# A gated FFT convolution followed by an MLP: two subtractions of its first part moved from GpSimd to VectorE

## The chip, the cores and the metric

The kernel runs on one core of one Trainium2 chip. The metric is the device time of one execution in microseconds. Each core has engines with a queue of their own, which take their instructions in the order of the program: TensorE (PE, with weight loads shown as PEld), VectorE (DVE), ScalarE (ACT), GpSimd (POOL), and SyncE (SP), which here issues nearly all DMAs. Data lie in SBUF; matrix products come out in PSUM, from where VectorE and ScalarE read them.

## The reference

Two stages. The first is a long convolution along the sequence with a filter that a small network makes from position embeddings; the second an MLP with ELU.

```python
def _attn_ref(x, v, pos_emb, w1, w2):            # x, v: 4 x 12480 x 128
    h_filt = (np.maximum(pos_emb @ w1, 0.0) @ w2) * np.exp(-0.01 * pos)[:, None]
    u = x * v
    Uf = np.fft.rfft(u, n=2 * S, axis=1)
    Hf = np.fft.rfft(h_filt, n=2 * S, axis=0)
    y = np.fft.irfft(Uf * Hf[None], n=2 * S, axis=1)[:, :S]
    return x * y

def _moe_ref(x, w_in, w_out):                    # 49920 x 128, 128 x 2048, 2048 x 128
    h = x @ w_in
    return np.where(h > 0, h, np.exp(np.minimum(h, 0)) - 1) @ w_out
```

## The kernel before

**Split numbers.** Products that need float32 accuracy are made from operands in a shorter format, `F32R`. An operand is split in two: the high part is a copy into `F32R`, the low part what the copy lost (`low = full - high`). `mm3` (L52 to L55) then does three matmuls: high by high (L53), low by high (L54) and high by low (L55). `copy` (L57) is always a ScalarE activation, so all high parts are shown at L58.

**The order of the work.** The schedule is written out by hand: each engine's queue holds its instructions in the order in which the Python code makes them. The transform over 12480 positions is done in two steps over 104 x 60. The kernel has three parts: `stage1` for batch 0 with `first=True`, in which the filter and the MLP's weights are prepared as well; `stage2` for batch 0 with `first=True`; and then the MLP over all batches, with `stage1` and `stage2` of batches 1 to 3 (with `first=False`) interleaved.

**The first part.** `stage1(..., first=True)` is a loop over 15 groups g, each with four steps i (r = i // 2, w = i % 2). What a group needs was prepared ahead:

- `load(g + 3)` at i = 0 (L182): two DMAs, `xt` and `vt`, of 416 KB each, in three buffers.
- `gate(g + 2)` at the group's start (L147): `vt = xt * vt`. It runs on VectorE for groups 0 and 1, on GpSimd afterwards (L101, L102).
- `split(g + 1)` at i = 1 (L184): `u_h` on ScalarE (L110), then `u_l = vt - u_h` (L112).

In each of its steps a group runs three matmuls `aps` from `u_h`, `u_l` (L158). Their result is copied out of PSUM by VectorE when w = 0 (L161) and by ScalarE when w = 1 (L163), and two steps together are stored by one DMA.

Between these lies the filter (class `Filter`), for q = 2g + r. `step(q + 3, 0)` transposes the embeddings (`pt`), `step(q + 2, 1)` multiplies by w1 (`rp`) and takes the Relu on ScalarE (`r_sb`, L236), `step(q + 1, 2)` multiplies by w2 (`hps`, L242), applies the window on VectorE (`h_sb`, L245), and splits: `h_h` on ScalarE (L252) and `h_l = h_sb - h_h` (L253). `transform(q)` runs twelve matmuls `Hps` on an earlier step's `h_h`, `h_l`, then combines on ScalarE (`hsb`, L266) and VectorE (L267).

At i = 1 `weights(c)` decodes 256 columns of the MLP's weights, which arrive as 64 bit numbers, with ten operations on VectorE (seven at L301, then L315, L317 and L318). `split_w(c - 1)` then splits the columns decoded one round earlier: the high part on ScalarE, the low part on GpSimd (L329). `split(g + 1)` follows.

So the queues hold, for one group:

| step | PE | VectorE | ScalarE | GpSimd |
| --- | --- | --- | --- | --- |
| start | | | | gate(g + 2) L102 |
| i = 0 | pt, aps, hps | L161, L245 | pt_sb, h_h | h_l L253 |
| i = 1 | rp, aps, Hps | L267, ten of weights | r_sb, a_sb, hsb, weights high, u_h | weights low L329, u_l L112 |
| i = 2 | pt, aps, hps | L161, L245 | pt_sb, h_h | h_l L253 |
| i = 3 | rp, aps, Hps | L267 | r_sb, a_sb, hsb | |

Before the loop, `gate(0)`, three rounds of `step`, `gate(1)` and `split(0)` come in this order. In `stage1` with `first=False` the choice at L111 is VectorE already.

Of the kernel before, what the change touches and what calls it, by code (L numbers as in the profile page):

```python
# [11 lines left out]
ALU = mybir.AluOpType  # L12
# [26 lines left out]
def fftconv_gate_elu_mlp_kernel(ctx: ExitStack, tc: tile.TileContext, x, v, pos_emb, w1, w2,  # L39
                                w_in, w_out, dft, ident, window, tab, out):  # L40
    nc = tc.nc
# [15 lines left out]
    def copy(out, in_):  # L57
        nc.scalar.activation(out=out, in_=in_, func=ACTF.Copy)  # L58
# [22 lines left out]
    def stage1(st, h, ps_pool, ps_tag, first):  # L81
# [22 lines left out]
        def split(g):  # L104
            if g >= NG:
                return
            vt = ld.pop(g)[1]
            u_h = up.tile([N1, 2, G, D], F32R, tag="u_h", name="u_h")
            u_l = up.tile([N1, 2, G, D], F32R, tag="u_l", name="u_l")
            copy(u_h, vt)  # L110
            e = nc.gpsimd if first and g else nc.vector  # L111
            e.tensor_tensor(out=u_l, in0=vt, in1=u_h, op=ALU.subtract)  # L112
            us[g] = (u_h, u_l)

# [18 lines left out]
        else:  # L133
# [6 lines left out]
            for _ in range(2 if h > 1 else 0):  # L140
                yield
        split(0)
        if not first:
            yield
        for g in range(NG):
# [3 lines left out]
            for i in range(4):  # L149
# [33 lines left out]
                if i == 1:  # L183
                    split(g + 1)  # L184
# [9 lines left out]
    class Filter:  # L194
# [25 lines left out]
        def step(self, g, q):  # L220
            if g >= NGF:
                return
            hp, psh = self.hp, self.psh
            if q == 0:
                p = self.pos.pop(g)
                pt = psh.tile([64, 2 * GF, N1], F32, tag="t", name="pt")
                for n in range(2 * GF):
                    nc.tensor.transpose(out=pt[:, n, :], in_=p[:, n // GF, n % GF, :], identity=id_sb[:N1, :N1])
                pt_sb = hp.tile([64, 2 * GF, N1], F32, tag="pt_sb", name="pt_sb", bufs=2)
                copy(pt_sb, pt)  # L230
                self.t[g] = pt_sb
            elif q == 1:
                rp = psh.tile([64, 2 * GF, N1], F32, tag="r", name="rp")
                nc.tensor.matmul(out=rp, lhsT=self.w1, rhs=self.t[g], start=True, stop=True)
                r_sb = hp.tile([64, 2 * GF, N1], F32, tag="r_sb", name="r_sb", bufs=2)
                nc.scalar.activation(out=r_sb, in_=rp, func=ACTF.Relu)  # L236
                self.t[g] = r_sb
            elif q == 2:
                r_sb = self.t.pop(g)
                hps = psh.tile([N1, 2, GF, D], F32, tag="h", name="hps")  # L240
                for n in range(2 * GF):
                    nc.tensor.matmul(out=hps[:, n // GF, n % GF, :], lhsT=r_sb[:, n, :], rhs=self.w2,  # L242
                                     start=True, stop=True)
                h_sb = hp.tile([N1, 2, GF, D], F32, tag="h_sb", name="h_sb", bufs=2)
                nc.vector.tensor_tensor(  # L245
                    out=h_sb, in0=hps,
                    in1=self.win[:, :, g * GF:(g + 1) * GF].rearrange("p w (n o) -> p w n o", o=1).to_broadcast([N1, 2, GF, D]),
                    op=ALU.mult)
                h_h = hp.tile([N1, 2, GF * D], F32R, tag="h_h", name="h_h", bufs=2)
                h_l = hp.tile([N1, 2, GF * D], F32R, tag="h_l", name="h_l", bufs=2)  # L250
                hv = h_sb.rearrange("p w n d -> p w (n d)")
                copy(h_h, hv)  # L252
                nc.gpsimd.tensor_tensor(out=h_l, in0=hv, in1=h_h, op=ALU.subtract)  # L253
                self.hs[g] = (h_h, h_l)

        def transform(self, g):
# [499 lines left out]
```

## Time and profile before

| | |
| --- | --- |
| median of 3 runs | 3546.19 us (3544.32 to 3550.76) |
| the profiled execution | 3553.1 us |
| its span, first to last instruction | 3551.3 us |
| mean granted TensorE clock | 0.981 |
| busy in the span: PE, DVE, ACT, POOL | 96%, 88%, 68%, 66% |
| DMA | 646.30 MB, mean 182 GB/s |

The span counts from the first instruction to the last; the execution's time has a little more around it. Busy shares are means over parts with different limits. The granted clock is the share of full speed at which TensorE was let run; it is 1.0 or 0.5 at any time, and means over a stretch lie between. In the rows below times are microseconds from the span's start, unless marked ns; a row of a timeline gives start, duration, engine, line, operation, output and inputs, and in brackets how long the engine sat idle before it and whose end released it.

### The profile page before, as it was taken

How to read it: one execution, taken by the hardware profiler on the slowest of the kernel's cores; microseconds unless marked ns; L12 is line 12 of the kernel's file. 1: busy time of each engine (PE TensorE's matmuls, PEld its weight loads, DVE VectorE, ACT ScalarE, POOL GpSimd, SP SyncE). 2: the span in 40 equal slices, each digit the busy share in tenths (PEclk: the TensorE clock that was granted, in tenths of full speed). 3: DMA queues.
4: the chain of work that ended last, by engine and by line, in shares of the span. 5: the costliest groups of instructions: out<-in, count | busy, mean ns of one | idle time of the engine just before them, and what ended most of it. 6: DMA issues, size and time to landing. Idle time of an engine off the chain costs nothing.

```text
span 3551.3 us, 53404 instructions
## 1 busy us (share of the span) xinstructions
PE 3394.7 (96%) x18444; PEld 3131.3 (88%) x18444; DVE 3114.3 (88%) x3897; ACT 2410.1 (68%) x3290; POOL 2355.2 (66%) x1622
## 2 busy tenths in 40 slices
PE   7978879999999999999999999999999999999999
PEld 5667758889989998889999998899999999999998
DVE  4549969999999989999999989999999988888887
ACT  3445548766666677876666677776666677777776
POOL 5758857667767766557677656666766656565565
PEclk9879979999999999999999999999999999999999
DMA  6758887667767616778888846778888832222221
GB/s 187 236 170 268 269 245 222 203 175 217 214 191 215 192 50 182 242 213 228 230 241 225 230 124 183 239 215 237 232 240 226 230 102 60 71 59 64 67 59 27
DMA packets 383995, 646.30 MB, mean 182 GB/s; under 512 B 24678, under 2 KB 170438, under 8 KB 374366
## 3 DMA queue, kind: packets, MB, share of 16 engines
q1 hardware_dynamic: 383305, 642.73, 63.8%
q8 instruction: 147, 2.41, 0.3%
q14 instruction: 122, 1.00, 0.1%
q10 hardware_dynamic: 421, 0.16, 0.0%
HBM read 412.76 MB, written 230.03 MB: 181 GB/s over the span
## 4 chain that ended last, share of the span: by engine, by line
PE 59%; DVE 10%; DMA 7%; issue 4%; ACT 1%; POOL 1%; SPq 1%; POOLq 0%; DVEq 0%; ACTq 0%
PE fps L53 8%; PE fps L55 8%; PE fps L54 8%; PE ops L53 7%; PE ops L54 7%; PE ops L55 7%; DMA al<-a_d 3%; DVE g_l L581 3%; PE bps L450 3%; DVE g L572 2%; DMA vt<-in_v_dram 2%; PE xps L53 2%; PE xps L55 2%; PE xps L54 2%; PE yps L53 1%
## 5 line engine op out<-in xcount | busy, mean ns | idle before, releaser
L575 POOL CAST g_h<-g 128x832 fp32r<-128x832 f32 x960 | 1228.3, 1283 | 961.0 <-DVE g L572 960.1
L565 ACT ACTIVATE n<-fps 128x832 f32<-128x832 f32 x960 | 831.9, 867 | 737.9 <-PE fps L55 725.1
L572 DVE SCALAR_TENSOR_TENSOR g<-n,fps 128x832 f32<-128x832 f32 x960 | 974.4, 1015 | 224.2 <-ACT n L566 218.2
L581 DVE TENSOR_TENSOR g_l<-g,g_h 128x832 fp32r<-128x832 f32 x960 | 1111.4, 1158 | 18.3 <-POOL g_h L575 18.3
L566 ACT ACTIVATE n<-n 128x832 f32<-128x832 f32 x960 | 864.6, 901 | 30.4
L53 PE MATMUL fps<-t_h,wi_h 128*128 128x416 f32 x1920 | 715.8, 373 | 22.1 <-DVE g L572 20.9
L53 PE MATMUL ops<-g_h,wo_h 128*128 128x416 f32 x1920 | 677.9, 353 | 0.8 <-ACT o_sb L58 0.3
L54 PE MATMUL ops<-g_l,wo_h 128*128 128x416 f32 x1920 | 675.2, 352 | 0.7 <-DVE g_l L581 0.7
L55 PE MATMUL fps<-t_h,wi_l 128*128 128x416 f32 x1920 | 675.8, 352 | 0.0
L55 PE MATMUL ops<-g_h,wo_l 128*128 128x416 f32 x1920 | 675.8, 352 | 0.0
L54 PE MATMUL fps<-t_l,wi_h 128*128 128x416 f32 x1920 | 675.0, 352 | 0.0
L431 POOL TENSOR_TENSOR p<-p 120x768 f32<-120x768 f32 x204 | 478.9, 2348 | 77.9 <-DVE p L425 58.4
L53 PEld LDWEIGHTS fps<-t_h,wi_h 128*128 128x128 f32 x1920 | 362.4, 189 | 55.9 <-DVE g L572 36.1
L54 PEld LDWEIGHTS fps<-t_l,wi_h 128*128 128x128 f32 x1920 | 364.4, 190 | 13.3 <-DVE t_l L554 0.3
L53 PEld LDWEIGHTS ops<-g_h,wo_h 128*128 128x128 f32 x1920 | 361.8, 188 | 7.1 <-POOL g_h L575 2.1
L54 PEld LDWEIGHTS ops<-g_l,wo_h 128*128 128x128 f32 x1920 | 362.5, 189 | 4.2 <-DVE g_l L581 1.4
L55 PEld LDWEIGHTS ops<-g_h,wo_l 128*128 128x128 f32 x1920 | 361.5, 188 | 4.1
L55 PEld LDWEIGHTS fps<-t_h,wi_l 128*128 128x128 f32 x1920 | 361.8, 188 | 3.2
L423 DVE TENSOR_TENSOR p<-xps,f 120x512 f32<-120x512 f32 x416 | 283.0, 680 | 14.1 <-DMA f<-f_d 5.1
L432 POOL TENSOR_TENSOR p<-p 120x256 f32<-120x256 f32 x204 | 249.5, 1223 | 16.0
L450 PE MATMUL bps<-p,t 120*120 120x256 f32 x832 | 220.4, 387 | 35.4 <-POOL p L432 26.6
L358 DVE TENSOR_TENSOR tl<-t,th 120x360 fp32r<-120x360 f32 x208 | 211.2, 1016 | 27.4 <-ACT th L58 27.3
(96 smaller groups left out, 4946.2 us busy)
## 6 DMA issues: line engine op xcount, KB each, us to landing
a_d<-a_sb SPq DMA_DIRECT2D x90, 832.0 KB
al<-a_d SPq DMA_DIRECT2D x156, 480.0 KB
f<-f_d SPq DMA_DIRECT2D x312, 240.0 KB
b_d<-b_sb SPq DMA_DIRECT2D x156, 480.0 KB
b<-b_d SPq DMA_DIRECT2D x90, 832.0 KB
t<-in_tab_dram SPq DMA_DIRECT2D x208, 281.2 KB
xt<-in_x_dram SPq DMA_DIRECT2D x60, 416.0 KB
vt<-in_v_dram SPq DMA_DIRECT2D x60, 416.0 KB
```

What stands on the lines that cost most here:

```text
L53: nc.tensor.matmul(out=ps, lhsT=hi, rhs=bh, start=start, stop=False)
L54: nc.tensor.matmul(out=ps, lhsT=hi, rhs=bl, start=False, stop=False)
L55: nc.tensor.matmul(out=ps, lhsT=lo, rhs=bh, start=False, stop=stop)
L423: nc.vector.tensor_tensor(out=p[:, :, :2], in0=ps[:, :, 0:1, :].to_broadcast([RI, TG, 2, D]), in1=f[:, :, r], op=ALU.mult)
L431: e.tensor_tensor(out=q, in0=q, in1=p, op=ALU.add)
L432: e.tensor_tensor(out=q[:, :, 1], in0=q[:, :, 1], in1=q[:, :, 2], op=ALU.add)
L450: nc.tensor.matmul(out=ps[:, o], lhsT=t[:, o, 3 * N2:], rhs=y[:, o, :2], start=True, stop=True)
L565: nc.scalar.activation(out=n, in_=ps[:, :, :NT], func=ACTF.Relu, scale=-1.0)
L566: nc.scalar.activation(out=n, in_=n, func=ACTF.Exp, scale=-1.0)
L572: nc.vector.scalar_tensor_tensor(out=g, in0=n, scalar=-1.0, in1=ps[:, :, :NT], op0=ALU.add, op1=ALU.max)
L575: nc.gpsimd.tensor_copy(out=g_h, in_=g)
L581: nc.vector.tensor_tensor(out=g_l, in0=g, in1=g_h, op=ALU.subtract)
```

## The change

The low part of `u` in the first part, groups 1 to 14, and the low part of the filter, 30 times, are computed by VectorE in place of GpSimd. Operands and results are the same, and each instruction keeps its place in the order of the program, now in VectorE's queue: `u_l` behind the ten operations of `weights`, `h_l` behind `h_sb` (L245). GpSimd keeps the gates (L102) and the weights' low parts (L329) in this part.

```diff
@@ split(g) in stage1
             copy(u_h, vt)
-            e = nc.gpsimd if first and g else nc.vector
+            e = nc.vector
             e.tensor_tensor(out=u_l, in0=vt, in1=u_h, op=ALU.subtract)
@@ step(g, 2) in Filter
                 copy(h_h, hv)
-                nc.gpsimd.tensor_tensor(out=h_l, in0=hv, in1=h_h, op=ALU.subtract)
+                nc.vector.tensor_tensor(out=h_l, in0=hv, in1=h_h, op=ALU.subtract)
```

## The prediction

> **What bounds the kernel now.** The profiled execution has a span of 3551.3 us and took 3553.1 us; the three timed runs have their median at 3546.19. The change touches only the first part, so I read stages by windows first, then who waits there, then one group as a timeline.
>
> ```profile
> 25.00:222.00 197.00, 182.63 (x908) 129.26 (x908) 105.15 (x238) 89.69 (x171) 147.24 (x71) 0.87 0.65 200
> ```
>
> The columns are stretch, length, busy time of PE, PEld, DVE, ACT and POOL, granted clock, DMA share and GB/s. The loop of 15 groups lasts from about 25 to 222 us. PE is busy 182.6 of 197 us, at a clock of 0.87; VectorE has 92 us free, GpSimd 50. DMA is no bound at 0.65. The next part starts with loads of what this one stores last, so a microsecond here is a microsecond of the whole.
>
> ```profile
> ACT h_h L58 <- DVE h_sb L245: 85.2, 30, 5.6
> PE aps L54 <- POOL u_l L112: 9.0, 10, 2.0
> ```
>
> Of the waits up to 240 us these two matter (sum in us, times, longest). PE waits 9.0 us for `u_l` from GpSimd: that is all the change can save directly. But ScalarE hangs on VectorE through `h_sb` 30 times, and VectorE is where the work goes.
>
> ```profile
> 81.40:92.90 11.50, 10.65 (x65) 7.58 (x64) 6.68 (x17) 6.12 (x14) 10.39 (x5) 1.00 0.85 268
> 92.90:106.35 13.45, 12.60 (x63) 9.38 (x63) 6.70 (x17) 6.26 (x13) 10.38 (x5) 0.80 0.81 259
> 106.35:121.05 14.70, 14.70 (x67) 10.23 (x65) 6.78 (x17) 6.38 (x13) 10.38 (x5) 0.72 0.71 226
> 132.60:148.20 15.60, 13.11 (x63) 9.39 (x63) 8.96 (x17) 6.25 (x13) 9.73 (x5) 0.80 0.72 225
> ```
>
> Each window is one group. At full clock it takes 11.5 us; a spell at half clock makes two neighbours 13.45 and 14.70, that is 28.15 - 2 x 11.52 = 5.1 us too long.
>
> ```profile
> 199.37 0.69 DVE L267 TENSOR_TENSOR hsb<-Hps,hsb 104x512 f32<-104x512 f32 x1 [3.02 <-ACT hsb L58]
> 199.72 3.02 POOL L329 TENSOR_TENSOR wo_l<-r,wo_h 128x256 fp32r<-128x256 f32 x1 [1.34 <-ACT wo_h L58]
> ...
> 202.18 0.85 DVE L318 TENSOR_TENSOR r<-r,k 128x256 f32<-128x256 f32 x1
> 202.70 2.56 POOL L112 TENSOR_TENSOR u_l<-vt,u_h 104x1024 fp32r<-104x1024 f32 x1
> 202.95 0.68 DVE L161 COPY a_sb<-aps 104x512 f32<-104x512 f32 x1
> 203.55 0.68 DVE L245 TENSOR_TENSOR h_sb<-hps,win_sb 104x512 f32<-104x512 f32 x1
> 204.26 0.63 ACT L58 ACTIVATE h_h<-h_sb 104x512 fp32r<-104x512 f32 x1 [3.28 <-DVE h_sb L245]
> 204.79 0.49 ACT L236 ACTIVATE r_sb<-rp 64x416 f32<-64x416 f32 x1
> 205.31 0.47 PE L54 MATMUL aps<-u_l,dft_h 104*104 104x512 f32 x1 [0.85 <-POOL u_l L112]
> 205.95 0.91 PEld L242 LDWEIGHTS hps<-w_sb,r_sb 64*104 64x104 f32 x8 [0.38 <-ACT a_sb L58]
> 206.28 0.69 DVE L267 TENSOR_TENSOR hsb<-Hps,hsb 104x512 f32<-104x512 f32 x1 [2.06 <-ACT hsb L58]
> ...
> 210.89 0.69 DVE L267 TENSOR_TENSOR hsb<-Hps,hsb 104x512 f32<-104x512 f32 x1 [2.72 <-ACT hsb L58]
> ```
>
> A clean group, L267 to L267, 11.52 us (start, length, engine, line). Two things meet at `hps` at 205.95. **One** is PE's own path, held 0.85 us at 205.31 by `u_l`, which left GpSimd at 205.26. **The other** is a chain through two queues: ten weight operations on VectorE up to L318, then L161, L245, then on ScalarE `h_h` and `r_sb`, which ends at 205.28 and feeds `hps`. It is only 0.7 us ahead of PE. Had PE not waited for `u_l`, `hps` would have started at 205.28 + 0.06, 5.97 after L267, and the rest, 210.89 - 205.95 = 4.94, would follow. So the group takes 10.9 + s, where s is whatever is put on VectorE ahead of L161.
>
> **The trace has tested this rule.**
>
> ```profile
> 132.44 0.69 DVE L267 TENSOR_TENSOR hsb<-Hps,hsb 104x512 f32<-104x512 f32 x1 [2.76 <-ACT hsb L58]
> 134.61 0.82 DVE L315 SCALAR_TENSOR_TENSOR r<-l,f 128x256 f32<-128x256 uint32 x1
> 135.11 2.57 POOL L112 TENSOR_TENSOR u_l<-vt,u_h 104x1024 fp32r<-104x1024 f32 x1
> 135.35 2.61 DVE L317 TENSOR_TENSOR k<-k,s 128x256 uint32<-128x256 uint32 x1
> 138.34 0.69 DVE L161 COPY a_sb<-aps 104x512 f32<-104x512 f32 x1
> ...
> 140.74 1.12 PE L242 MATMUL hps<-w_sb,r_sb 64*104 64x128 f32 x8 [2.29 <-ACT r_sb L236]
> ```
>
> Here L161 starts 5.90 after L267 instead of 3.58, so s = 2.32, and `hps` should start 5.97 + 2.32 = 8.29 after it; it starts at 8.30, PE now waiting for `r_sb`. What caused it: L317, two SBUF operands and 256 elements, took 2.61 us and ended when GpSimd's `u_l` did. The two engines don't run such operations side by side.
>
> **The change, part by part.** Durations:
>
> ```profile
> L112 DVE TENSOR_TENSOR u_l<-vt,u_h x46: 1208/1565/2457, 26.5 to 2334.8; 104x1024 fp32r<-104x1024 f32 x46
> L395 DVE TENSOR_TENSOR a_l<-al,a_h 120x512 fp32r<-120x512 f32 x1 | 0.7, 691 | 2.9 <-ACT a_h L58 2.9
> L253 POOL TENSOR_TENSOR h_l<-h_sb,h_h x30: 1264/1276/1514, 25.6 to 221.3; 104x512 fp32r<-104x512 f32 x30
> L102 POOL TENSOR_TENSOR vt<-xt,vt x12: 2346/2366/2559, 50.6 to 191.7; 104x1024 f32<-104x1024 f32 x12
> ```
>
> *`h_l`, 30 times, cost nothing.* It leaves GpSimd (1.28 us) and takes about 0.69 on VectorE, by the row of `a_l`, of equal width. In the queue it stands behind L245 and waits there for `h_h`, ready at 204.89; it would run to 205.6, while the next, L267, comes at 206.28 after 2.06 us of idling. Behind the waiting `h_l` are L267 and the next L161, both later anyway. If that cover were gone, 30 x 0.6 = 18 us. Before the loop the first `h_l` now precedes the second gate and the first `u_l`: between nothing and 0.63 + 0.69 = 1.3 us; I take 0.6.
>
> *`u_l`, 14 times, is on the chain.* It stands between L318 and L161. Alone it takes 1.21 us, less the 0.08 by which successive records overlap: s = 1.13 and a group of 12.03, **+0.5 us**. PE's 9.0 us of waiting for `u_l` are in this balance: `r_sb` is simply late instead.
>
> *The gate, moved without being edited.* On GpSimd the next operation behind L329 was `u_l`; now it is the gate L102 of a later group, and it reads SBUF too. It would ask for its operands in the same place, while L318 runs, and compete with VectorE's `u_l`. At 135.11 GpSimd's operation, recorded 0.32 before L315's end, went ahead of the following L317. At 202.70 it is 0.33 before L318's end. The opposite case exists:
>
> ```profile
> 598.44 1.54 DVE L112 TENSOR_TENSOR u_l<-vt,u_h 104x1024 fp32r<-104x1024 f32 x1
> 599.43 3.75 POOL L529 TENSOR_TENSOR b<-b,b 104x1024 fp32r<-104x1024 f32 x1 [0.53 <-ACT b L58]
> 599.90 1.01 DVE L581 TENSOR_TENSOR g_l<-g,g_h 128x832 fp32r<-128x832 f32 x1
> ```
>
> There VectorE's next operation ran at once and GpSimd waited. If the gate goes first, it ends where `u_l` did, at 205.26, and VectorE's `u_l` ends four times 0.28 later (L317, with a quarter of its elements, ended 0.28 after GpSimd at 137.68): 206.38. L161 starts 0.08 before that, at 206.30: s = 3.35, a group of 14.2, **+2.7 us**. [...]
>
> Is the gate ready by then?
>
> ```profile
> 99.99 1.62 SPq L94 DMA_DIRECT2D vt<-in_v_dram  x1
> 106.53 3.00 POOL L329 TENSOR_TENSOR wi_l<-r,wi_h 128x256 fp32r<-128x256 f32 x1 [2.99 <-ACT wi_h L58]
> 113.25 2.37 POOL L102 TENSOR_TENSOR vt<-xt,vt 104x1024 f32<-104x1024 f32 x1
> ```
>
> Its loads are issued at 99.99; with the store ahead of them they are 1.25 MB, about 5 us at 259 GB/s, so they land between 105 and 113.25, and L329 ends at 109.53. The trace leaves it open; I count half of the groups each way. The first and the last two have no such gate.
>
> *The clock.* PE's gap at `hps` grows from 0.85 to about 1.5 us, with the gate first to over 3.
>
> ```profile
> 213.70:217.10 3.40, 1.85 (x14) 1.49 (x13) 2.05 (x3) 1.32 (x3) 3.40 (x3) 1.00 0.31 91
> 217.10:222.00 4.90, 4.90 (x18) 3.60 (x17) 1.98 (x3) 1.90 (x4) 1.61 (x2) 0.50 0.58 162
> ```
>
> PE idled 1.55 of 3.4 us, and 0.50 was granted next; in the group from 81.40 it idled 0.85 and kept 1.00. Clock 0.87 over the loop is some 50 us at half, about five spells. I add two, at 2.4 (15.60 less 10.9 + 2.32) to 5.1 us: +7. At half clock PE is last (14.70 above 14.2), and the chain is hidden.
>
> **The sum.** Three uncontested groups 3 x 0.5 = 1.5; of eleven contested four late gates, 2.0, four early ones, 10.8, three hidden by half clock, 0; clock 7; head 0.6: **+22 us**. On the profiled execution that is 3575; on the median **3568 us**.
>
> **Rivals.** *The gate always goes first* (chance 0.2): 11 x 2.7 + 1.5 + six more spells at 3.5 = +52, 3598. For it speaks 135.11, against it 598.44. *The gate always comes too late, no more spells* (0.2): 11 x 0.5 = +6, 3552, no change. *Hidden altogether* (0.08): half clock or DMA sets the pace; 3546; the DMA share of 0.65 speaks against it. *Faster* (0.1): `u_l` is ready sooner, PE's gap closes and spells go. That decides where s is below 0.62 (11.52 - 10.9), or where spells fall away by luck of their timing: 9 us of waits and two or three spells, -19, 3527. Against it stand 1.13 for s and the 8.30 at 140.74. [...]
>
> **How the numbers follow.** The forecast has 0.42. About 0.2% (7 us) is what a measurement can tell from no change. Slower by more: forecast, first rival and a little of the second, 0.65; same 0.24; faster 0.11. The range takes in the late gate, less one spell, and most of the always early gate: 3547 to 3595.
>
> **What would show it.** Right: group windows of 12 to 14 us at full clock, PE waiting at `hps` for `r_sb` and no longer at L54; VectorE's `u_l` at 1.2 or 3.3 us, the long ones ending 1.1 after a gate; `h_l` followed by an idle VectorE; a clock below 0.87. Wrong: groups under 11.5 us, or L161 starting within 3.6 us of L267.

## The result and the profile after

| | us |
| --- | --- |
| before, median of 4 runs | 3548.48 (3544.32 to 3559.18) |
| after, median of 4 runs | 3592.74 (3589.06 to 3595.22) |
| ratio of after to before, 95% interval | 1.0119 (1.0094 to 1.0144) |
| forecast, range | 3568, 3547 to 3595 |

The kernel became 44 us slower. The direction was right and the time lies inside the range, but the forecast loss of 22 us was half of the real one; the time is near that of the first rival, in which the gate always goes first (3598).

The first fence is from the page of after, the second holds windows of after: the stretch behind the loop, the eleven contested groups together, one of them, and the two clock stretches within it (columns as in the prediction).

```profile
span 3590.2 us, 53421 instructions
```

```profile
262.00:3590.20 3328.20, 3202.34 (x17512) 2996.91 (x17510) 3008.75 (x3658) 2316.94 (x3114) 2211.36 (x1547) 0.99 0.64 181
53.70:240.10 186.40, 157.92 (x698) 111.06 (x697) 125.31 (x209) 68.89 (x133) 60.81 (x22) 0.75 0.56 176
121.35:138.30 16.95, 13.82 (x65) 9.64 (x65) 11.41 (x19) 6.26 (x13) 5.54 (x2) 0.80 0.56 164
...
124.90:131.60 6.70, 3.57 (x27) 2.79 (x25) 5.32 (x5) 1.98 (x5) 2.34 (x1) 1.00 0.17 54
131.70:138.40 6.70, 6.70 (x24) 4.78 (x23) 2.61 (x5) 2.66 (x6) 0.00 (x0) 0.50 0.80 205
```

The same two windows of before:

```profile
222.00:3551.30 3329.30, 3203.43 (x17511) 2997.66 (x17510) 3006.34 (x3656) 2315.93 (x3112) 2207.79 (x1548) 0.99 0.64 181
...
54.20:199.40 145.20, 136.15 (x698) 96.68 (x696) 76.32 (x177) 68.75 (x133) 113.83 (x56) 0.85 0.71 222
```

Behind the loop nothing changed: 3328 against 3329 us. The whole loss is in the first part, and nearly all of it in the eleven contested groups, 186.4 against 145.2 us: 16.95 a group instead of 13.2. GpSimd's busy time fell by half, VectorE's rose by 49 us (an operation that is held up counts as busy for all of its time, as the 3.40 us of `u_l` below), and PE did the same 698 matmuls in 41 us more.

The timeline of after shows one such group, the answer to the clean group of before:

```profile
121.35 0.69 DVE L267 TENSOR_TENSOR hsb<-Hps,hsb 104x512 f32<-104x512 f32 x1 [4.15 <-ACT hsb L58]
121.70 3.02 POOL L329 TENSOR_TENSOR wi_l<-r,wi_h 128x256 fp32r<-128x256 f32 x1 [12.23 <-ACT wi_h L58]
...
124.16 0.84 DVE L318 TENSOR_TENSOR r<-r,k 128x256 f32<-128x256 f32 x1
124.68 2.56 POOL L102 TENSOR_TENSOR vt<-xt,vt 104x1024 f32<-104x1024 f32 x1
124.92 3.40 DVE L112 TENSOR_TENSOR u_l<-vt,u_h 104x1024 fp32r<-104x1024 f32 x1
128.25 0.68 DVE L161 COPY a_sb<-aps 104x512 f32<-104x512 f32 x1
128.38 0.47 PE L54 MATMUL aps<-u_l,dft_h 104*104 104x512 f32 x1 [1.52 <-DVE u_l L112]
...
130.28 0.69 DVE L253 TENSOR_TENSOR h_l<-h_sb,h_h 104x512 fp32r<-104x512 f32 x1 [0.76 <-ACT h_h L58]
130.70 1.22 PE L242 MATMUL hps<-w_sb,r_sb 64*104 64x128 f32 x8 [1.61 <-ACT r_sb L236]
...
131.64 0.69 DVE L267 TENSOR_TENSOR hsb<-Hps,hsb 104x512 f32<-104x512 f32 x1 [0.67 <-ACT hsb L58]
...
138.30 0.69 DVE L267 TENSOR_TENSOR hsb<-Hps,hsb 104x512 f32<-104x512 f32 x1 [3.33 <-ACT hsb L58]
```

The gate is recorded at 124.68, right where GpSimd's `u_l` used to be, 0.32 before L318's end. VectorE's `u_l` takes 3.40 us and ends at 128.32, 1.08 after the gate's end at 127.24. That is what is called a collision below. L161 starts 6.90 after L267, s = 3.32. PE waits twice, 1.52 us for `u_l` and 1.61 for `r_sb`, and in the following 6.7 us its clock is 0.50, which stretches the other half of the group. All eleven contested `u_l` look like that; the three without a gate behind L329 take 1.21 to 1.22. The first and the last of the eleven in after's timeline:

```profile
57.23 3.39 DVE L112 TENSOR_TENSOR u_l<-vt,u_h 104x1024 fp32r<-104x1024 f32 x1
...
225.94 3.41 DVE L112 TENSOR_TENSOR u_l<-vt,u_h 104x1024 fp32r<-104x1024 f32 x1
```

### The profile page after: what moved, and what is told of

It reads as the page before. It is cut to its first block, busy times and chain, and to the rows that moved or that the text cites. A ratio compares the mean times of both kernels' runs of the same rounds, so it can differ in the third digit from the quotient of the medians.

```text
span 3590.2 us, 53421 instructions
## 1 busy us (share of the span) xinstructions
PE 3410.5 (95%) x18444; PEld 3141.6 (88%) x18444; DVE 3171.2 (88%) x3941; ACT 2410.0 (67%) x3290; POOL 2286.3 (64%) x1578
## 3 DMA queue, kind: packets, MB, share of 16 engines
q8 instruction: 147, 2.41, 0.3%
## 4 chain that ended last, share of the span: by engine, by line
PE 67%; DVE 13%; DMA 8%; issue 5%; POOL 3%; ACT 2%; SPq 1%; POOLq 0%; ACTq 0%; DVEq 0%
PE fps L53 8%; PE fps L55 8%; PE fps L54 8%; PE ops L53 8%; PE ops L54 7%; PE ops L55 7%; PE bps L450 4%; DMA al<-a_d 4%; DVE g_l L581 3%; DMA vt<-in_v_dram 2%; DVE g L572 2%; PE xps L53 2%; DVE u_l L112 2%; PE xps L55 2%; PE xps L54 2%
## 5 line engine op out<-in xcount | busy, mean ns | idle before, releaser
L581 DVE TENSOR_TENSOR g_l<-g,g_h 128x832 fp32r<-128x832 f32 x960 | 1111.5, 1158 | 19.8 <-POOL g_h L575 19.8
L423 DVE TENSOR_TENSOR p<-xps,f 120x512 f32<-120x512 f32 x416 | 282.5, 679 | 14.2 <-ACT a_h L58 6.7
```

What stands on the lines that cost most here:

```text
L423: nc.vector.tensor_tensor(out=p[:, :, :2], in0=ps[:, :, 0:1, :].to_broadcast([RI, TG, 2, D]), in1=f[:, :, r], op=ALU.mult)
L581: nc.vector.tensor_tensor(out=g_l, in0=g, in1=g_h, op=ALU.subtract)
```

## The experiments

The theory after the result was this: the gate's turn on GpSimd is the cost, together with the half clock that PE's gaps bring on. The main rival was: VectorE's longer queue is the cost, whatever GpSimd does. Where the expectations say lock or port, this is what the traces show of it: with a gate recorded beside it `u_l` takes 3.37 to 3.41 us, without one 1.21 to 1.22; what in the chip holds it up, no run shows. Each ratio below is to the kernel before, run on the same chip.

| run | median us (runs) | ratio to before, 95% interval |
| --- | --- | --- |
| `u_l` alone moved | 3553.13 (10) | 1.0013 (1.0000 to 1.0025) |
| `h_l` alone moved | 3543.87 (10) | 0.9987 (0.9972 to 1.0002) |
| changed kernel, loads issued later | 3557.40 (10) | 1.0019 (1.0005 to 1.0032) |
| changed kernel, split made earlier | 3530.26 (10) | 0.9953 (0.9938 to 0.9968) |
| changed kernel, gates on VectorE | 3557.94 (5) | 1.0041 (1.0026 to 1.0056) |
| changed kernel, more work on PE | 3563.72 (4) | 1.0048 (1.0032 to 1.0063) |

### `u_l` alone

Of the change only this part (against before):

```diff
-            e = nc.gpsimd if first and g else nc.vector
+            e = nc.vector
```

> Only u_l goes to VectorE; h_l stays on GpSimd, where it now stands between L329 and the gate and has to wait for h_h. Theory (what costs is the gate taking GpSimd's turn behind L329 and holding VectorE's u_l off): the gate comes too late to collide, u_l takes 1.21 us in all 14 groups, L161 starts 4.7 us after L267, a group takes 12.0 us at full clock, and the kernel some 7 to 14 us more than before: 3555 to 3563 us, a ratio of 1.002 to 1.004 to before. Rival (u_l behind the weight operations costs what was measured whoever shares the port): u_l or the wait behind it still 3.3 us, 3585 to 3593 us.

Measured: 3553.13 us, 2 us below the theory's 3555 to 3563, and 32 us short of the rival. A clean group in this run's timeline:

```profile
132.04 0.69 DVE L267 TENSOR_TENSOR hsb<-Hps,hsb 104x512 f32<-104x512 f32 x1 [3.47 <-ACT hsb L58]
...
135.62 1.21 DVE L112 TENSOR_TENSOR u_l<-vt,u_h 104x1024 fp32r<-104x1024 f32 x1
136.76 0.68 DVE L161 COPY a_sb<-aps 104x512 f32<-104x512 f32 x1
...
138.78 1.26 POOL L253 TENSOR_TENSOR h_l<-h_sb,h_h 104x512 fp32r<-104x512 f32 x1 [3.35 <-ACT h_h L58]
139.15 1.12 PE L242 MATMUL hps<-w_sb,r_sb 64*104 64x128 f32 x8 [1.34 <-ACT r_sb L236]
140.01 2.37 POOL L102 TENSOR_TENSOR vt<-xt,vt 104x1024 f32<-104x1024 f32 x1
...
144.09 0.69 DVE L267 TENSOR_TENSOR hsb<-Hps,hsb 104x512 f32<-104x512 f32 x1 [2.11 <-ACT hsb L58]
```

The gate stands behind a waiting `h_l` and comes at 140.01, more than 3 us after `u_l`. So `u_l` takes 1.21, L161 starts 4.72 after L267, `hps` waits for `r_sb`, and the group takes 12.05 us, where the prediction's rule gave 12.03. At full clock the move of `u_l` itself costs what was forecast. Four of the eleven contested groups of this run are like that; the other seven met half clock and took 13.4 to 14.7 us.

### `h_l` alone

The other part (against before):

```diff
-                nc.gpsimd.tensor_tensor(out=h_l, in0=hv, in1=h_h, op=ALU.subtract)
+                nc.vector.tensor_tensor(out=h_l, in0=hv, in1=h_h, op=ALU.subtract)
```

> Only h_l goes to VectorE; u_l stays on GpSimd behind L329, and the gate comes right behind u_l. Theory (h_l hides in VectorE's idle time ahead of L267): as before within 0.2%, 3541 to 3556 us. Rival (the gate, now next behind u_l, goes ahead of the waiting h_l and holds it and L267 up for 1.2 to 1.8 us a group): 3565 to 3575 us, h_l at 2 to 3 us in most groups of i = 2.

Measured: 3543.87 us, no difference that the interval can tell. From the list of this tile's instructions, with the shortest, median and longest of 30 in ns:

```profile
L253 DVE TENSOR_TENSOR h_l<-h_sb,h_h x30: 691/693/845, 26.7 to 208.2; 104x512 fp32r<-104x512 f32 x30
```

`h_l` is not held up by a gate, the longest takes 0.85 us, and it hides as forecast. So the parts cost 1.0013 and 0.9987 by themselves, and together 1.0119. The loss belongs to neither edit: it appears only when both leave GpSimd, because the waiting `h_l` was what kept the gate away from `u_l`.

### The gate made late

The changed kernel with the loads issued two steps later; `if first` concerns this part alone:

```diff
-                if i == 0:
+                if i == (2 if first else 0):
                     load(g + (3 if first else 2))
```

> The changed kernel, with the loads of a group issued two steps later (i = 2 instead of i = 0), so that the gate's data land only after u_l has started; the engines' work is the same. Theory (the lock, decided by when the gate is ready): u_l 1.21 us in most groups, L161 4.7 us after L267, gates start after u_l; 3555 to 3568 us. Rival (VectorE's longer queue is the cost, the gate's time doesn't matter): 3585 to 3597 us as the changed kernel. Third: the gate comes so late that u_h waits for it: above 3597 us.

Measured: 3557.40 us, as the theory has it. Nothing moved between engines against the changed kernel, and of its 1.0119 only 1.0019 is left, some 35 us less. In the list of waits between 53 and 230 us it is now GpSimd that waits, for the gate's data:

```profile
POOL vt L102 <- DMA vt<-in_v_dram: 36.8, 9, 4.7
```

All contested `u_l` take 1.21 us. The groups are not 12.0 us, though: windows of two neighbours in this run,

```profile
67.50:81.15 13.65, 12.04 (x66) 8.90 (x64) 9.22 (x20) 6.16 (x13) 5.37 (x2) 0.87 0.75 219
81.15:94.80 13.65, 12.05 (x66) 8.91 (x64) 9.22 (x20) 6.15 (x13) 5.37 (x2) 0.87 0.75 223
```

show 13.65 each, with a clock of 0.87: PE idles 1.6 us in each group (13.65 less the 12.04 and 12.05 busy), and some of each is at half clock.

### The split made earlier

Both low parts on VectorE, but the next group's split at i = 0, around the filter's own: `u_h` ahead of `h_h`, `u_l` between `h_sb` and `h_l` (against the changed kernel; `split_hi` and `split_lo` are the two halves of `split`):

```diff
         def step(self, g, q, between=None):
...
                 copy(h_h, hv)
+                if between:
+                    between()
                 nc.vector.tensor_tensor(out=h_l, in0=hv, in1=h_h, op=ALU.subtract)
...
-                        filt.step(q + 1, 2)
+                        if i == 0:
+                            split_hi(g + 1)
+                            filt.step(q + 1, 2, lambda: split_lo(g + 1))
+                            if q + 1 >= NGF:
+                                split_lo(g + 1)
+                        else:
+                            filt.step(q + 1, 2)
...
-                if i == 1:
+                if i == 1 and not first:
                     split(g + 1)
```

> Both low parts on VectorE as in the changed kernel, but u_h and u_l of the next group are made at i = 0 instead of i = 1: u_h on ScalarE ahead of h_h, u_l on VectorE between h_sb and h_l, in its idle time ahead of L267. Nothing is then put between L318 and L161 and PE no longer waits for u_l: s = 0, a group of 10.9 us at full clock, hardly any gap on PE and few spells at half clock. Theory: 25 us less than before, 3515 to 3540 us. Rival (something else is late next, ScalarE with u_h ahead of r_sb or VectorE with three operations in one gap): 3540 to 3556 us, as before.

Measured: 3530.26 us, ratio 0.9953 to before: faster than both kernels, and inside the theory's range. Windows of this run, one group and a longer stretch:

```profile
87.78:98.75 10.97, 10.50 (x66) 7.58 (x64) 9.79 (x20) 6.04 (x13) 5.38 (x2) 1.00 0.85 280
```

```profile
80.00:170.00 90.00, 85.75 (x528) 62.30 (x527) 79.38 (x155) 48.36 (x96) 43.94 (x18) 1.00 0.83 273
```

With nothing between L318 and L161 the group takes 10.97 us, where the rule 10.9 + s gives 10.9 for s = 0, and with PE idle for 0.47 us in the group (10.97 less 10.50 busy) no half clock came: 90 us at 1.00. VectorE is busier than in any group of before, 9.8 of 11.0 us. That it carries the work was never the trouble; where it carries it was.

### All gates on VectorE

```diff
-            e = nc.vector if first and g < 2 else nc.gpsimd
+            e = nc.vector if first else nc.gpsimd
             e.tensor_tensor(out=vt, in0=xt, in1=vt, op=ALU.mult)
```

> The changed kernel with all 13 remaining gates moved to VectorE too, so that GpSimd holds nothing but the weights' low parts in this part; VectorE carries 1.1 us more a group. Theory (the cost is the collision with the gate, not VectorE's load): u_l 1.21 us throughout; the gate stands between L267 and L161 of the next group, which makes the chain 12.0 + 1.1 = 13.1 us a group against 14.2 with the collision, before the clock's part: 3560 to 3580 us, faster than the changed kernel though VectorE does more. Rival (VectorE's load is the cost): slower than the changed kernel, 3600 to 3615 us.

Measured: 3557.94 us, 2 us below the theory's range and far from the rival: VectorE carries more than in the changed kernel, and the ratio is 1.0041 instead of 1.0119, some 28 us less. A group in windows of this run:

```profile
95.78:109.44 13.66, 12.05 (x66) 8.91 (x64) 10.36 (x20) 6.15 (x13) 3.02 (x1) 0.88 0.70 227
```

It takes 13.66 us with a clock of 0.88, as the group with late loads does, although I had reckoned its chain 1.1 us longer (13.1). The collision as the cost is confirmed; the 13.1 were wrong, and the second half of this group shows why, in the rows of VectorE and in a window from L267 to L267:

```profile
103.89 0.69 DVE L267 TENSOR_TENSOR hsb<-Hps,hsb 104x512 f32<-104x512 f32 x1 [0.67 <-ACT hsb L58]
104.49 1.22 DVE L102 TENSOR_TENSOR vt<-xt,vt 104x1024 f32<-104x1024 f32 x1
...
109.44 0.69 DVE L267 TENSOR_TENSOR hsb<-Hps,hsb 104x512 f32<-104x512 f32 x1 [1.08 <-ACT hsb L58]
```

```profile
103.89:109.44 5.55, 5.55 (x26) 4.21 (x24) 3.71 (x5) 2.50 (x6) 0.00 (x0) 0.69 0.70 187
```

PE is busy in all of the 5.55 us and sets the pace. The gate takes idle time of VectorE, of which 1.08 us are left; the run with late loads has 2.22 at the same place and the same 5.56 us. So the gate is not on the chain there. Whether it would be at full clock, no group of this run shows.

### More work on PE

The changed kernel with twelve matmuls more in each of groups 1 to 12, whose results the real ones overwrite:

```diff
+                if first and i == 0 and 0 < g < NG - 2:
+                    for _ in range(8):
+                        nc.tensor.matmul(out=ps, lhsT=dft_h[:, f, :], rhs=u_h[:, w], start=True, stop=True)
                 mm3(ps, dft_h[:, f, :], dft_l[:, f, :], u_h[:, w], u_l[:, w])
...
+                for _ in range(4 if fill is not None else 0):
+                    nc.tensor.matmul(out=hps.rearrange("p w n d -> p (w n d)"), lhsT=dft_h[:, 0, :],
+                                     rhs=fill[:, 0], start=True, stop=True)
                 for n in range(2 * GF):
                     nc.tensor.matmul(out=hps[:, n // GF, n % GF, :], lhsT=r_sb[:, n, :], rhs=self.w2,
```

> The changed kernel with work added on PE alone: in groups 1 to 12, eight more matmuls ahead of the first aps and four ahead of the first hps, overwritten by the real ones, 12 x 0.22 us a group at full clock, placed where PE waits for u_l and for r_sb. Theory (of the 44 us lost, some 15 to 25 are the half clock that PE's gaps bring on): the collisions stay (u_l 3.4 us), the clock over the loop rises from 0.79 to 0.9 or more, groups come down from 16.9 towards 14.2 us and the kernel is faster with more work, 3565 to 3582 us. Rival (the clock is a side effect and costs nothing of its own): 3590 us or more, 3595 to 3625 if the added work lands on the path.

Measured: 3563.72 us, 1 us below the theory's range, and 1.0048 to before where the changed kernel has 1.0119: with 144 matmuls added it is some 25 us faster. Windows of this run over the eleven groups, and over two neighbours:

```profile
51.90:209.30 157.40, 152.41 (x830) 106.82 (x828) 117.98 (x210) 67.31 (x133) 63.73 (x22) 0.97 0.65 205
```

```profile
97.98:112.30 14.32, 13.74 (x78) 9.45 (x76) 11.43 (x20) 6.04 (x13) 5.55 (x2) 1.00 0.64 196
112.30:125.53 13.23, 13.23 (x78) 9.60 (x76) 9.47 (x19) 6.14 (x13) 6.01 (x2) 1.00 0.78 243
```

The clock is 0.97 against 0.75, and a group with a collision takes 14.3 us: that is its price without the clock (the prediction had 14.2). What I did not expect is the second group. The timeline has these rows in the two:

```profile
101.55 3.42 DVE L112 TENSOR_TENSOR u_l<-vt,u_h 104x1024 fp32r<-104x1024 f32 x1
...
108.21 0.33 SPq L93 DMA_DIRECT2D xt<-in_x_dram  x1
...
112.65 3.01 POOL L335 TENSOR_TENSOR wi_l<-r,wi_h 128x256 fp32r<-128x256 f32 x1 [8.76 <-ACT wi_h L58]
115.86 1.21 DVE L112 TENSOR_TENSOR u_l<-vt,u_h 104x1024 fp32r<-104x1024 f32 x1
116.34 3.00 POOL L102 TENSOR_TENSOR vt<-xt,vt 104x1024 f32<-104x1024 f32 x1 [0.69 <-DMA vt<-in_v_dram]
```

(L335 is L329 of the other kernels, and L324 their L318.) Here the gate still waits for its data when GpSimd is free at 115.66, and `u_l` goes ahead of it. Four of the eleven collisions are gone, against my expectation that all would stay: there `u_l` takes 1.21 us and the gate is recorded after it. For two of these gates the trace names the DMA of their data as what they waited for, for the other two (143.59 and 185.49) L324 on VectorE, so that late data are less sure there. Part of the gain comes from these four groups, whose 13.2 us are just PE's work, the added one included.

## Why the prediction was right or wrong

**The chain 10.9 + s was right** at full clock, at each of three s: 10.97 at s = 0, 12.05 at 1.13, 14.3 at 3.3.

**That `h_l` costs nothing was right**: moved alone it made no difference, and in the changed kernel it follows an idle VectorE (the row at 130.28).

**The price of a collision was right**: 2.7 us was forecast, and 14.3 - 11.5 = 2.8 was measured at full clock.

**The step that failed is "I count half of the groups each way"**, and with it the three groups booked as hidden by half clock. All eleven collided, and one was hidden, this group of after:

```profile
88.81:103.61 14.80, 14.80 (x67) 10.35 (x66) 11.36 (x20) 6.15 (x13) 5.50 (x2) 0.71 0.50 149
```

PE is busy throughout, and it takes about what a half-clock group of before took (14.70), so the prediction's mechanism of hiding exists; the other ten took 16.4 to 17.8 us. The sum had 2.0 + 10.8 + 0 = 12.8 us for the eleven; at the full-clock price they come to 11 x 2.8 = 31.

Why the gate was always ready can be read from the time between a load's issue (L93) and the end of L329. In the run with more work on PE, at full clock, it has two values. In the five groups behind a collision it is 7.4 to 7.5 us, as from 108.21 to 115.66, and four of these five gates came 0.4 to 0.7 us late. In the four groups behind a late gate it is 8.6, and all four collided. The late gates started 7.8 to 8.1 us after the issue; the fifth was ready in time. In the changed kernel the distance is 9.5 to 10.9 us in ten of the eleven groups, each with half clock inside, and 8.0 in one at full clock (98.98 to 106.97), which was enough too. Its timeline has, in one of the ten, the load for the gate of 124.68 at

```profile
113.80 0.33 SPq L93 DMA_DIRECT2D xt<-in_x_dram  x1
...
121.70 3.02 POOL L329 TENSOR_TENSOR wi_l<-r,wi_h 128x256 fp32r<-128x256 f32 x1 [12.23 <-ACT wi_h L58]
```

which makes 124.72 - 113.80 = 10.9 us; the half clock lies just in this stretch. So the two costs feed each other: a collision makes a gap on PE (1.52 and 1.61 us in the group shown), half clock follows (0.50 in the 6.7 us from 131.70), half clock gives the loads time (9.5 to 10.9 us, where full clock had 7.4 to 7.5 behind a collision), and the next gate is early again. The first gate needs no half clock for it: its distance is 10.4 us in the changed kernel and in the run at full clock alike. This loop of causes is read from the traces; the run with PE's gaps filled speaks for it (0.97 against 0.75), but no run took the half clock away without adding work to PE. The prediction took the clock and the gate's readiness as two independent terms, and counted on half clock to hide three collisions.

**The clock's term was too small.** It had +7 us. In the changed kernel the eleven groups lose 186.4 - 11 x 14.3 = 29 us to it; before they lost 145.2 - 11 x 11.52 = 18, the one collision included. That is 11 more, with a clock of 0.75 against 0.85. It is what remains when every collision is put at its full-clock price, the hidden one included.

**The rest**: the three uncontested groups were booked at +1.5. L161 starts 4.7 us after L267 in the last two, as forecast, but the three together took 39.2 us against 41.7 before, 2.5 less. Part of that is the start's slow spell, which ended at another place: the `Hps` matmuls take 0.41 us instead of 0.28 up to 46.3 in before, and in after up to 38.2. The windows count this first spell as full clock, so the 0.87 that the prediction read for the loop was somewhat too high. The first L267 of the loop came at 39.02 instead of 37.77, 1.25 later, within the head's bounds of 0 to 1.3. That this is a cost of the change is not shown: the four runs on top of the changed kernel, with the same work ahead of the loop, have that L267 at 37.2 to 37.6.

**The sum as measured**, between these two traces: 31 + 11 - 2.5 + 1.3 = 41 in the first part; the two spans differ by 39.

**The rivals.** That the gate always goes first was right in mechanism and nearly in price. Its chance of 0.2 was too low: of the two rows that were weighed, the one at 135.11 had the changed kernel's very arrangement, a GpSimd operation right behind another and 0.32 us before the end of a short VectorE operation, and the one at 598.44 had not. It should have weighed more. In the changed kernel eleven of eleven gates, each recorded 0.24 to 0.25 us ahead of `u_l`, went first. To be recorded first was not always enough: the row at 598.44 stays unexplained (GpSimd's L529, recorded 0.47 ahead of L581, took 3.75 us where its median is 2.41, and L581 took 1.01), and L329, recorded at 121.70, ahead of VectorE's first weight operation at 121.96, took 3.02 us, where the one at 268.81, with no weight operations beside it, took 0.73. The faster rival's mechanism exists: PE's gap can be closed and the spells go, as the earlier split shows with 3530 us. The change as made does not do it.

## What to carry to other kernels

When an operation leaves an in-order queue, look at what moves up into its place and what that will meet; a waiting operation may have been keeping two others apart, and then two edits that cost next to nothing each can cost 1.2% together. Put work on a busy engine where it idles, not where it is free on average: the kernel with `u_l` between the weights and `a_sb` lost 44 us, and the one with `u_l` a step earlier won 17. Where a clock answers to gaps, as it seemed to here (0.75 over the eleven groups, 0.97 with matmuls put into PE's gaps), a gap costs more than its length, and terms that act through it can't be added as if they were independent.

## What the runs showed of the hardware

PE's half clock came and went on a fixed grid in both traces. In before it begins at 60.09, 101.05, 142.01 and 179.56 and lasts 10.24, 13.65, 6.83 and 13.65 us; in after it begins at 53.08, 63.32, 80.39 and 111.11 and lasts 6.83, 6.83, 17.07 and 10.24. Each length, and each distance between two of these starts in a trace, is a whole multiple of 3.413 us. The groups with late loads repeat at 13.65 us and those with the gates on VectorE at 13.66, which is four times 3.41, although their work differs; by their clocks of 0.87 and 0.88 some 3.3 to 3.5 us of each are at half clock. So the time of a group settled on the grid there. Gaps of 1.55 us in 3.40 were followed by half clock (in before, PE busy 1.85 of the 3.40 us from 213.70, 0.50 in the next 4.90).

That VectorE and GpSimd don't run operations such as L317 and `u_l` side by side the prediction took from one L317, which has 2.61 us where the median of its 16 in before is 0.42. In after, the eleven `u_l` beside a gate have 3.37 to 3.41 us, where the three others of the loop have 1.21 to 1.22.

GpSimd is held up too: L329 is recorded with 3.02 us behind VectorE's seven weight operations at L301 and the two that follow, and ends 0.55 to 0.57 after L318's start in group after group. The last L329 of after, at 268.81, which has no weight operations beside it, takes 0.73. Why it ends no sooner, no run here shows.
